# A second product of layer 2 by seven block products, with tokens in halves and two groups of PSUM banks that change parts

## The chip, the cores and the metric

The kernel runs on one core of one Trainium2 chip. The metric is device time in microseconds, the median over several runs. The engines are named as in the profile: PE (TensorE, the matmuls; PEld its weight loads), DVE (VectorE), ACT (ScalarE), POOL (GpSimd) and SP (SyncE, which issues most DMAs).

## The reference

Attention over 4 batches of 8 heads (576 tokens, head size 64) keeps only scores within tau of a row's maximum. Its output, 2304 tokens of 512 features, goes through two feed-forward layers with d_ff = 2048. q, k, v are float32; the weights of both layers arrive in 64 bits.

```python
scores = scale * np.matmul(q, k.transpose(0, 1, 3, 2))
thresh = np.max(scores, axis=-1, keepdims=True) - tau
scores = np.where(scores >= thresh, scores, -1000000000.0)
...
x = attn_out.transpose(0, 2, 1, 3).reshape(B * S, H * D)
h = x @ w_in;  r = np.maximum(h, 0.0);  x = (r * r) @ w_out      # layer 1
h = x @ w_in;  g = np.maximum(0.01 * h, h);  out = g @ w_out     # layer 2
```

## The kernel before

Attention runs first, 144 steps of one tile of queries each (functions `step`, `rest`, `values`). Between its matmuls stands the first part of layer 1 (`ffn`), 256 tokens at a time over 12 of the 16 blocks of d_ff. When attention is done, the second part of layer 1 (`h_unit`, `y_unit`) runs with 512 tokens at a time: the last 512 tokens over all of d_ff, and the rest over the remaining four blocks. Layer 2 comes last.

Layer 2 works on blocks of tokens: four of 512 and one of 256. d_ff is taken in eight pairs p of 128-wide blocks. Every operand is scaled by a power of two and split into a high and a low float16 half, and a product is three matmuls: high by high, high by low, low by high. The first product of layer 2 (`h_unit2`, line 986) already uses a scheme with seven block products in place of eight: the matrices are cut into 2 x 2 blocks, sums and differences of the blocks are multiplied, and the results are added up. Per (block, p) it has 7 products of 2 x 3 matmuls. Its four PSUM banks a, c, d, b are filled, copied or added out by ACT and DVE (lines 991 and 994), and a, c and d are added onto a second time. The activation is done by ACT on the result (lines 1014 and 1015), once to float16 and once in place, and DVE takes the difference as the low half (line 310).

The second product (`y_unit2`, line 1048) is plain: for each of four groups of 128 tokens (two in the small block) and each of the two halves of the pair, three matmuls of 512 columns, all accumulated over the eight pairs in four PSUM banks; at the last pair ACT scales a bank out (line 1052) and SP stores it.

The weights of layer 2 are loaded, converted from 64 bits, scaled and split while the second part of layer 1 runs (`single`, `bound`, `w_in2`, `w_out2`); `w_in2` also makes the sums and differences of blocks, `w_out2` only splits. `x_load2` reads layer 1's result back from DRAM, scales it and makes the seven blocks of x.

Nothing of this is in the order of the code: each call adds operations to a `Plan`, with priorities, buffers and, for some, several engines to choose from. `Plan.order` sorts them into one fixed order per engine by a table of costs (`price`, and the functions `act`, `dve`, `mm`), and each engine then works through its queue in that order.

## Time and profile before

| | us |
|---|---|
| median of 3 runs | 1037.73 |
| lowest and highest run | 1036.74, 1037.76 |
| the profiled execution | 1040.98 |
| its span in the trace | 1039.2 |
| PE busy (matmuls) in the span | 1001.7 |
| DVE, ACT, POOL busy | 714.4, 679.3, 370.4 |

The profiled execution is 3.25 us longer than the median. Busy times are unions over the span; idle time of an engine costs something only where another waits for it. The stages, as the trace shows them: attention with the first part of layer 1 until about 518 us, the second part of layer 1 until about 687 us, layer 2 until the end.

### The profile page before, as it was taken

To read this page: it belongs to the slowest core of one execution; us is meant where nothing else is said; L and a number is where in the kernel's file an instruction comes from. 1 tells how busy PE (TensorE), PEld (TensorE's weight loads), DVE (VectorE), ACT (ScalarE), POOL (GpSimd) and SP (SyncE) were. 2 spreads that over 40 slices of the span, in tenths; PEclk is the share of its full clock that TensorE was granted. 3 is DMA by queue.
4 is the path that set the end of the run, shared out by engine and by line. 5 is a ranking of instruction groups with operands and counts; after the bars stand their busy time and mean duration, and the time that the engine had idled before them with its cause. 6 is when DMAs were issued, how large, how long until landed. Compare 5 with 4: busy or idle time off the path is not lost.

```text
span 1039.2 us, 19111 instructions
## 1 busy us (share of the span) xinstructions
PE 1001.7 (96%) x6835; PEld 788.6 (76%) x6835; DVE 714.4 (69%) x1589; ACT 679.3 (65%) x1280; POOL 370.4 (36%) x482
## 2 busy tenths in 40 slices
PE   7899899999989989999999999999999999999998
PEld 4555588888989889899988898876666666666665
DVE  5988649879999877873766699996346346335333
ACT  5877787977776788875666697875455455444344
POOL 5787777975866878861200000000000000000000
PEclk9999999999999999999999999999999999999999
DMA  6554538988889996976576554331011010010010
GB/s 179 155 149 134 161 87 155 201 145 182 171 155 184 148 180 131 154 118 183 165 218 196 176 181 161 120 104 42 1 41 42 1 42 21 1 42 1 1 42 21
DMA packets 186990, 119.25 MB, mean 115 GB/s; under 512 B 146064, under 2 KB 164624, under 8 KB 186896
## 3 DMA queue, kind: packets, MB, share of 16 engines
q1 hardware_dynamic: 186528, 117.82, 48.1%
q8 instruction: 54, 0.88, 0.3%
q14 instruction: 40, 0.33, 0.1%
q10 hardware_dynamic: 368, 0.21, 0.1%
HBM read 70.98 MB, written 17.83 MB: 85 GB/s over the span
## 4 chain that ended last, share of the span: by engine, by line
PE 60%; DMA 2%; ACT 1%; POOL 0%; issue 0%; DVE 0%; DVEq 0%; ACTq 0%; POOLq 0%
PE y L1048 18%; PE h L986 16%; PE y L1109 8%; PE h L1067 8%; PE h L716 4%; PE y L742 4%; DMA PT<-P 2%; PE o L663 1%; PE s L565 1%; ACT e L576 0%; DVE e L582 0%; ACT r L723 0%; ACT tmp L678 0%; PE h L882 0%; ACT P L299 0%
## 5 line engine op out<-in xcount | busy, mean ns | idle before, releaser
L576 ACT ACTIVATE e<-s,nb 128x576 f32<-128x576 f32 x144 | 105.9, 740 | 57.7 <-DVE nb L575 38.1
L565 PE MATMUL s<-KH,Q 128*128 128x288 f32 (+1 forms) x440 | 123.3, 374 | 13.9 <-DVE e L582 9.8
L575 DVE TENSOR_REDUCE nb<-s 128x1 f32<-128x576 f32 x144 | 107.5, 750 | 33.6 <-PE s L565 32.9
L582 DVE SCALAR_TENSOR_TENSOR e<-s,th,e 128x576 f32<-128x576 f32 x144 | 116.7, 811 | 18.0 <-ACT e L576 11.4
L565 PEld LDWEIGHTS s<-KH,Q 128*128 128x128 f32 (+1 forms) x440 | 74.6, 186 | 33.0 <-issue 10.6
L1048 PEld LDWEIGHTS <-gl 128*128 128x128 f16 x432 | 42.3, 98 | 51.0
L875 POOL MEMSET xl<- 128x128 f32 x5 | 1.0, 205 | 221.8 <-issue 78.2
L629 DVE SCALAR_TENSOR_TENSOR P<-e,r,P 128x576 f16<-128x576 f32 x78 | 72.9, 943 | 7.2 <-ACT P L596 3.6
L1048 PEld LDWEIGHTS <-gh 128*128 128x128 f16 x432 | 41.9, 98 | 42.3
L663 PE MATMUL o<-PT,V 128*128 128x320 f16 (+1 forms) x396 | 57.5, 287 | 7.7 <-DVE xs L683 3.0
L565 PE MATMUL s<-KL,Q 128*128 128x288 f32 x200 | 55.8, 294 | 0.0
L663 PEld LDWEIGHTS <-V 128*128 128x128 f16 x396 | 35.4, 98 | 19.2 <-issue 6.6
L1014 ACT ACTIVATE gh<-r 128x512 f16<-128x512 f32 (+1 forms) x40 | 23.5, 588 | 40.1 <-DVE r L994 39.8
L312 POOL TENSOR_TENSOR gl<-r,gh 128x512 fp32r<-128x512 f32 x33 | 45.5, 1378 | 10.4 <-ACT gh L299 10.3
L310 DVE TENSOR_TENSOR xl<-xr,xh 128x512 f16<-128x512 f32 (+3 forms) x61 | 41.5, 684 | 10.9 <-ACT xh L299 10.5
L577 POOL TENSOR_SCALAR th<-nb,ca 128x1 f32<-128x1 f32 x85 | 36.2, 426 | 34.6 <-DVE nb L575 30.2
L1015 ACT ACTIVATE r<-r 128x512 f32<-128x512 f32 (+1 forms) x80 | 46.9, 586 | 2.2
L991 ACT COPY b0ih<-h 128x256 f32<-128x256 f32 (+1 forms) x40 | 14.0, 350 | 52.1 <-PE h L986 51.8
L994 DVE TENSOR_TENSOR b0ol<-h,b0oh 128x256 f32<-128x256 f32 (+1 forms) x20 | 7.9, 397 | 56.4 <-PE h L986 56.4
L585 POOL TENSOR_SCALAR t<-sum 128x1 f32<-128x1 f32 x82 | 33.9, 413 | 34.5 <-DVE e L582 29.7
L299 ACT CAST xh<-xr 128x512 fp32r<-128x512 f32 (+3 forms) x61 | 35.2, 582 | 15.1 <-DVE xr L310 10.8
L299 ACT CAST gh<-r 128x512 fp32r<-128x512 f32 (+1 forms) x66 | 40.3, 611 | 4.2 <-DVE r L1075 3.0
(919 smaller groups left out, 3281.1 us busy)
## 6 DMA issues: line engine op xcount, KB each, us to landing
wraw<-w SPq DMA_DIRECT2D x64, 512.0 KB, 4.4
wraw<-qT SPq DMA_DIRECT2D x20, 288.0 KB, 4.1
wraw<-kT SPq DMA_DIRECT2D x20, 288.0 KB, 4.2
out<-yo SPq DMA_DIRECT2D x18, 256.0 KB, 2.0
VA<-vv SPq DMA_DIRECT2D x32, 128.0 KB, 2.8
x2d<-yo SPq DMA_DIRECT2D x16, 256.0 KB, 2.7
xr<-x2d SPq DMA_DIRECT2D x4, 1024.0 KB, 5.4
y1d<-ys SPq DMA_DIRECT2D x14, 256.0 KB, 2.5
```

Of the source, the lines that this page charges most:

```text
L299: alts.append(("A", act(n, psum), lambda: nc.scalar.copy(o(), i()), kind))
L565: nc.tensor.matmul(ps.get()[r, g, 0:S2], lhsT=o.Q.get()[:, q], rhs=(kk.get() if o.KL else f32(kk.get()))[:, g_(g)], start=k == 0 or not o. ...
L575: op(("V", 0.75, lambda: nc.vector.tensor_reduce(out=nb.get(), in_=pv(), axis=AX.XY, op=ALU.max, negate=True)), [ps], [nb], i + CFG["pd1"] ...
L576: op(("A", 0.74, lambda: nc.scalar.activation(e.get(), pv(), AF.Exp, bias=nb.get(), scale=1.0)), [ps, nb], [e], i + CFG["pex"], True)
L582: op(("V", 0.82, lambda: nc.vector.scalar_tensor_tensor(out=e.get(), in0=pv(), scalar=th.get(), in1=e.get(), op0=ALU.is_ge, op1=ALU.mult, ...
L629: op(("V", 0.8, lambda: nc.vector.scalar_tensor_tensor(out=lo(), in0=ev(), scalar=r_.get()[:, k:k + 1], in1=hi(), op0=ALU.mult, op1=ALU.su ...
L663: nc.tensor.matmul(ps.get()[:, 0:w], lhsT=o.V16.get()[:, k if k < NH else k - NH, h].rearrange("p a d -> p (a d)"), rhs=parts16(pt)[:, k, ...
L986: nc.tensor.matmul(ps.get()[:, 0:w], lhsT=half(wt)[:, c0 + kc * P:c0 + (kc + 1) * P], rhs=xt(k)[:, kc], start=fresh and q == 0, stop=q == ...
L1015: op(("A", act(n), lambda rv=rv: nc.scalar.activation(rv(), rv(), AF.Prelu, scale=GK, alpha=0.01)), [r], [r], pr)
L1048: nc.tensor.matmul(y.get()[:, 0:DM], lhsT=l, rhs=r, start=(first and a == 0 and q == 0), stop=(last and a == 1 and q == 2))
L1067: nc.tensor.matmul(ps.get()[:, 0:n], lhsT=a.get()[:, kc * P:(kc + 1) * P], rhs=x.get()[:, kc, 0:n], start=(q == 0 and kc == 0), stop=(q == ...
L1109: nc.tensor.matmul(o(), lhsT=l, rhs=r, start=(first and q == 0), stop=(last and q == 2))
```

## The change

The second product of layer 2 also becomes seven block products. For 256 tokens and a pair p, g is a 2 x 2 matrix of blocks of 128 tokens by 128 of d_ff, and w_out a 2 x 2 matrix of blocks of 128 of d_ff by 256 features. Three of the blocks of g and three of the weights are used as they are, and four sums and differences of each are made (`h_unit2` for g, `spread` for the weights, which now serves both weight matrices). Seven products of three matmuls of 256 columns are accumulated over all eight pairs into seven half banks of four PSUM banks; only at the end are they joined, by one activation of ACT and seven operations of DVE, to two tiles of 128 tokens.

A block of 512 tokens is two such halves s of 256 tokens, and together they need eight banks, while the first product needs four of the eight that there are. So the first half is accumulated while the first product runs, in the other group of four banks, two pairs behind it; the blocks of g of the second half are kept in SBUF for all eight pairs (`g_tiles`, in tiles that are free by then), and the second half runs behind the last first product, in the banks that it used. Then the two groups change parts for the next block. The blocks of x are made between (`x_load2`, the scale now earlier in `x_stat`), into one buffer that is free only when the block's last first product is done. The activation is one instruction in place for each (block, p). The numbers of the planner's table are others, and `wold` has a third entry; GK, a power of two, keeps the sums of blocks in the range of float16.

In the diff, long lines stand whole and other parts are left out.

```diff
-GK = 2.0 ** -6
+GK = 2.0 ** -8
...
-           {'V': 2.331, 'A': 0.3, 'G': 0.438},
-           {'V': 2.518, 'A': 1.239, 'G': 2.454}],
+           {'V': 2.871, 'A': 0.393, 'G': 0.481},
+           {'V': 2.901, 'A': 1.503, 'G': 2.396},
...
+    def spread(p, g, y, keep, alone, mix, labels, fit, pr):
...
+        x0, sh, sl = (tile_of(room.pop(0)) for _ in range(3))
+        if p % 2 == 0:
+            rare[g] = tile_of(room.pop(0))
+        x2, c2 = rare[g], p % 2 * DM
+        quarter = lambda k: lambda: f32(y[k // 2].get())[:, k % 2 * h:(k % 2 + 1) * h]
+        halves((x0, 0), (x0, 2 * h), lambda: f32(y[keep].get()), 2 * h, [y[keep]], pr)
+        halves((x2, c2), (x2, c2 + h), quarter(alone), h, [y[alone // 2]], pr)
+        for o_, a_, b_, alu in mix:
+            op(tt(quarter(o_), quarter(a_), quarter(b_), h, alu), [y[a_ // 2], y[b_ // 2]], [y[o_ // 2]], pr)
         for k in range(2):
+            halves((sh, 2 * k * h), (sl, 2 * k * h), lambda k=k: f32(y[k].get()), 2 * h, [y[k]], pr)
+        room.extend(f"w{p}{'io'[g]}{k}" for k in "hl")
...
-        hi, lo = (tile_of(room.pop(0)) for _ in range(2))
-        for a, v in enumerate(y2v[1, p]):
-            op(fitted(lambda v=v: f32(v.get()), DM, fit), [v, fit], [v], pr)
-            halves((hi, a * DM), (lo, a * DM), lambda v=v: f32(v.get()), DM, [v], pr)
+        WO[p] = spread(p, 1, y2v[1, p], 1, 0, [(0, 1, 0, ALU.subtract), (1, 3, 1, ALU.subtract), (3, 3, 0, ALU.subtract), (2, 2, 3, ALU.subtract)], ("23", "1", "5746"), fit, pr)
...
+    def g_tiles(j, p, s):
+        if s == 0:
+            hi, lo = val("fb", "gh2", 3, [P, TB], F32R), val("fb", "gl2", 3, [P, TB], F32R)
+            return lambda: half(hi), lambda: half(lo), hi, lo
+        if p < 3:
+            t = val("stage", "wraw", CFG["wrb"], [P, 2 * S], F32)
+            return lambda: half(t)[:, 0:2 * DM], lambda: half(t)[:, 2 * DM:4 * DM], t, t
+        if p == 3:
+            hi, lo = (val("fb", "ya", 2, [P, TB], F32) for _ in range(2))
+            return lambda: half(hi), lambda: half(lo), hi, lo
...
-        op(tt(lambda: r2.get()[:, hi], u2, tm, w, ALU.add), [u2v, tmv, f], [r2], pr)
-        out = []
-        for r, ring in ((r1, "gh2"), (r2, "gl2")):
-            g = val("fb", ring, 3, [P, TB], F32R)
-            rv = lambda r=r: r.get()[:, 0:n]
-            op(("A", act(n), lambda g=g, rv=rv: nc.scalar.activation(half(g)[:, 0:n], rv(), AF.Prelu, scale=GK, alpha=0.01)), [r], [g], pr)
-            op(("A", act(n), lambda rv=rv: nc.scalar.activation(rv(), rv(), AF.Prelu, scale=GK, alpha=0.01)), [r], [r], pr)
-            op(sub(lambda g=g: half(g)[:, TB:TB + n], rv, lambda g=g: half(g)[:, 0:n], n), [r, g], [g], pr)
-            out.append(g)
-        G2[j, p] = out
...
+        op(tt(dest(1, 1), ta, tb, w, ALU.add), [av, bv, e], [r], pr)
+        ns = 1 + two
+        allr, alls = (lambda v=v: v.get()[:, 0:ns * 4 * P].rearrange("p (s k q) -> p s k q", s=ns, k=4) for v in (r, sv))
+        op(("A", act(ns * 4 * P), lambda: nc.scalar.activation(r.get()[:, 0:ns * DM], r.get()[:, 0:ns * DM], AF.Prelu, scale=GK, alpha=0.01)), [r], [r], pr)
+        a21, a11, a22, a12 = (lambda k=k: allr()[:, :, k] for k in range(4))
+        s1, s2, s3, s4 = (lambda k=k: alls()[:, :, k] for k in range(4))
+        op(tt(s1, a21, a22, ns * P, ALU.add), [r], [sv], pr)
+        op(sub(s3, a11, a21, ns * P), [r], [sv], pr)
+        op(sub(s2, s1, a11, ns * P), [r, sv], [sv], pr)
+        op(sub(s4, a12, s2, ns * P), [r, sv], [sv], pr)
+        p3, p7 = slice(0, 3 * P), slice(3 * P, 7 * P)
+        for s in range(ns):
+            hi, lo, hv, lv = g_tiles(j, p, s)
+            ps_ = pr + CFG["sp"] * s
+            br = lambda s=s: r.get()[:, s * DM + P:(s + 1) * DM]
+            sr = lambda s=s: sv.get()[:, s * DM:(s + 1) * DM]
+            op(rnd(lambda hi=hi: hi()[:, p3], br, 3 * P, engs="AVG"), [r], [hv], ps_)
+            op(rnd(lambda hi=hi: hi()[:, p7], sr, 4 * P, engs="AVG"), [sv], [hv], ps_)
+            op(sub(lambda lo=lo: lo()[:, p3], br, lambda hi=hi: hi()[:, p3], 3 * P), [r, hv], [lv], ps_)
+            op(sub(lambda lo=lo: lo()[:, p7], sr, lambda hi=hi: hi()[:, p7], 4 * P), [sv, hv], [lv], ps_)
+            G2[j, p, s] = hi, lo, [hv] if lv is hv else [hv, lv]
...
-            for m in range(nm):
-                Y[m] = val("ps_y", "y", 4, [P, 512], F32)
-        for m in range(nm):
-            y = Y[m]
-            for a, g in enumerate(gs):
-                def prod(m=m, a=a, g=g, y=y):
-                    gh, gl = (half(g)[:, k * TB + m * P:k * TB + (m + 1) * P] for k in range(2))
-                    vh, vl = (half(t)[:, a * DM:(a + 1) * DM] for t in (wh, wl))
+            pool, ring = banks[bank]
+            YS[j, s] = [val(pool, ring, 4, [P, 512], F32) for _ in range(4)]
+        ps = YS[j, s]
+        for y, ks in zip(ps, ("16", "72", "45", "3")):
+            vs = list(dict.fromkeys(t for k in ks for t in (WO[p][k][0], WO[p][k][2])))
+            def prod(y=y, ks=ks):
+                for c, k in enumerate(ks):
+                    wh, c0, wl, c1 = WO[p][k]
+                    gh, gl = (g()[:, piece[k] * P:(piece[k] + 1) * P] for g in (hi, lo))
+                    vh, vl = half(wh)[:, c0:c0 + h], half(wl)[:, c1:c1 + h]
                     for q, (l, r) in enumerate(((gh, vh), (gh, vl), (gl, vh))):
-                        nc.tensor.matmul(y.get()[:, 0:DM], lhsT=l, rhs=r, start=(first and a == 0 and q == 0), stop=(last and a == 1 and q == 2))
-                op(("T", 3 * mm(DM), prod), [wh, wl, g], [y], pr)
-            if last:
-                yo = val("fb", "yo", 2, [P, TB], F32)
-                op([("A", act(DM, True, True), lambda y=y, yo=yo: nc.scalar.activation(yo.get(), y.get(), AF.Copy, scale=us.get())),
-                    ("V", dve(DM, ap=True), lambda y=y, yo=yo: nc.vector.tensor_scalar(out=yo.get(), in0=y.get(), scalar1=us.get(), scalar2=None, op0=ALU.mult))], [y, us], [yo], pr)
-                dma(lambda m=m: out[t0 + m * P:t0 + (m + 1) * P, :], lambda yo=yo: yo.get()[:, 0:DM], [yo], [], pr, P * DM * 4)
+                        nc.tensor.matmul(y.get()[:, c * h:(c + 1) * h], lhsT=l, rhs=r, start=first and c == 0 and q == 0, stop=last and c == len(ks) - 1 and q == 2)
+            op(("T", 3 * len(ks) * mm(h), prod), vs + gv, [y], pr)
+        if not last:
+            return
+        top, low = (val("fb", "yo", 2, [P, TB], F32) for _ in range(2))
+        b0, b1, b2, b3 = ps
+        part = lambda t, c: lambda: t.get()[:, c * h:(c + 1) * h]
+        def join(o, ov, y, c, x, xv):
+            op(("V", dve(h, ap=True), lambda: nc.vector.scalar_tensor_tensor(out=o(), in0=part(y, c)(), scalar=us.get(), in1=x(), op0=ALU.mult, op1=ALU.add)), [y, us, xv], [ov], pr)
+        op(("A", act(h, True, True), lambda: nc.scalar.activation(part(top, 0)(), part(b0, 0)(), AF.Copy, scale=us.get())), [b0, us], [top], pr)
+        join(part(top, 1), top, b0, 1, part(top, 0), top)
+        join(part(low, 0), low, b1, 0, part(top, 1), top)
+        join(part(top, 0), top, b1, 1, part(top, 0), top)
+        join(part(low, 1), low, b2, 1, part(low, 0), low)
+        join(part(top, 1), top, b2, 1, part(top, 1), top)
+        join(part(low, 0), low, b2, 0, part(low, 0), low)
+        join(part(top, 1), top, b3, 0, part(top, 1), top)
+        r0 = t0 + s * 2 * P
+        for k, t in enumerate((low, top)):
+            dma(lambda k=k: out[r0 + k * P:r0 + (k + 1) * P, :], lambda t=t: t.get(), [t], [], pr, P * DM * 4)
...
+    for j in range(len(blocks)):
+        two, more = blocks[j][1] == TB, j + 1 < len(blocks)
+        for p in range(NU + 2):
+            if more and p == CFG["xp"]:
+                x_stat(j + 1, T0 + 2 * t, banks[bh])
+            if p < NU:
+                need(WI, p, t)
+                h_unit2(j, p, T0 + 2 * t, bh)
+                t += CFG["th"] * (2 if two else 1)
+            if p > 1:
+                need(WO, p - 2, t)
+                y_unit2(j, p - 2, 0, T0 + 2 * t, by)
+                t += CFG["th"]
+        if more:
+            x_load2(j + 1, T0 + 2 * (t - CFG["x2l"]))
+        if two:
+            for p in range(NU):
+                y_unit2(j, p, 1, T0 + 2 * t, bh)
+                t += CFG["th"]
+            bh, by = by, bh
```

Where the instructions stand. First PE in layer 2 of before, inside a step of the second block: the end of the first product (h banks) and the start of the second (y banks); gh and gl are tiles of g, w1ih, w1oh and so on tiles of weights.

```order
L986 LDWEIGHTS w1il
L986 MATMUL h_10952<-xh_9710,w1il 128x256
L1048 LDWEIGHTS gh_10900
L1048 MATMUL y<-w1oh,gh_10900 128x512
L1048 LDWEIGHTS gh_10900
L1048 MATMUL y<-w1ol,gh_10900 128x512
```

Each load serves a matmul of 512 columns. Now PE inside a second product of the changed kernel, in its first block (w2ol, w3ol and w4oh hold weights, gh and gl the high and low halves of g's blocks).

```order
L1133 LDWEIGHTS gh_9616
L1133 MATMUL y<-w2ol,gh_9616 128x256
L1133 LDWEIGHTS gl_9674
L1133 MATMUL y<-w2ol,gl_9674 128x256
L1133 LDWEIGHTS gh_9616
L1133 MATMUL y<-w3ol,gh_9616 128x256
L1133 LDWEIGHTS gh_9616
L1133 MATMUL y<-w4oh,gh_9616 128x256
```

The matmuls of the second product are 256 wide and alternate between high and low tiles of g. The change of parts of the banks: PE at the end of the first block, where the second half ends in h banks (its g kept in xl_9697) and the first product of the second block begins in y banks.

```order
L1133 LDWEIGHTS xl_9697
L1133 MATMUL h_9798<-r_8969,xl_9697 128x256
L1055 LDWEIGHTS w8ih
L1055 MATMUL y<-xh_9741,w8ih 128x256
L1055 LDWEIGHTS w8ih
L1055 MATMUL y<-xh_9741,w8ih 128x256
L1055 LDWEIGHTS w8ih
L1055 MATMUL y<-xl_9762,w8ih 128x256
```

Three first products follow here, 126 matmuls, before the first second product of that block. Next DVE in one step of before, in the second block: b0il is a tile of partial sums, r the result of the first product, gh and gl the tiles of g.

```order
L994 TENSOR_TENSOR b0il<-h_9572,b0ih 128x256
L994 TENSOR_TENSOR r_9602<-h_9588,b0ih 128x256
L994 TENSOR_TENSOR r_9602<-h_9563,b0il 128x256
L994 TENSOR_TENSOR r_9616<-h_9572,b0il 128x256
L310 TENSOR_TENSOR r_9616<-b0il 128x256
L310 TENSOR_TENSOR gh_9611<-r_9602,gh_9611 128x512
L310 TENSOR_TENSOR gl_9623<-r_9616,gl_9623 128x512
```

That is five operations of 256 columns and two of 512. DVE in one step of the changed kernel's second block: b_9016 and b_9059 are two wide tiles that hold partial sums and the blocks of g, wraw is one of the tiles in which the second half's g is kept.

```order
L1063 TENSOR_TENSOR b_9016<-y,b_9016 128x256
L329 TENSOR_TENSOR gl_10212<-b_9059,gh_10162 128x384
L329 TENSOR_TENSOR gl_10212<-b_9016,gh_10162 128x512
L329 TENSOR_TENSOR wraw<-b_9059,wraw 128x384
L1063 TENSOR_TENSOR b_9059<-y,b_9016 128x256
L329 TENSOR_TENSOR wraw<-b_9016,wraw 128x512
L329 TENSOR_TENSOR b_9016<-b_9059 128x2x128
L1063 TENSOR_TENSOR b_9059<-y,b_9016 128x256
L329 TENSOR_TENSOR b_9016<-b_9059 128x2x128
L1063 TENSOR_TENSOR b_9059<-y,b_9016 128x256
L329 TENSOR_TENSOR b_9016<-b_9016,b_9059 128x2x128
L329 TENSOR_TENSOR b_9059<-b_9016 128x256
```

Steps are interleaved here: a step has 4 additions from PSUM, 1 sum, 4 block sums (2x128 columns each; the last follows below these rows), and for each half a subtraction of 384 and one of 512. Counted over the whole order: of the pieces of layer 2's weights on DVE, 30 of 512 and 33 of 256 columns stood between the start of layer 1's second part and the first addition of layer 2, and 35 and 59 stand there now; behind it 10 and 7 stood, and 13 and 21 stand now. In attention, PE's order is the same row by row until the second product with w10 of `ffn`'s fourth block of tokens, which the trace of before has at about 425 us. Of attention's steps, POOL makes the low half of P by a subtraction (line 312) in 27 instead of 17, DVE by its fused operation (line 629) in 69 instead of 78.

## Rows read from the trace of the kernel before

**Rows 1.** Windows: length, busy us of PE, PEld, DVE, ACT, POOL; clock, DMA share, GB/s
```profile
0.00:345.00 345.00, 317.86 (x2175) 256.37 (x2176) 289.01 (x666) 259.47 (x455) 254.34 (x332) 0.99 0.74 157
345.00:400.00 55.00, 51.15 (x405) 47.83 (x405) 42.40 (x98) 43.01 (x75) 43.76 (x56) 1.00 0.93 173
...
518.00:687.00 169.00, 169.00 (x818) 141.81 (x818) 135.85 (x278) 125.35 (x255) 4.63 (x10) 1.00 0.54 170
687.00:1036.00 349.00, 348.33 (x2511) 231.69 (x2509) 162.89 (x378) 168.55 (x346) 1.81 (x5) 1.00 0.07 25
```

**Rows 2.** Waits of PE, 345 to 520 us (us in total, times, longest)
```profile
PE s L565 <- DVE e L582: 2.0, 4, 0.7
...
PE y L742 <- POOL gl L312: 0.3, 1, 0.3
```

**Rows 3.** Chain that ended last (start us, us, what)
```profile
697.06 4.58 PE h L986 x42
701.64 5.18 PE y L1048 x24
...
998.20 2.35 PE h L986 x42
1000.54 2.59 PE y L1048 x12
```

**Rows 4.** Costliest groups: weight loads of the two products (busy, mean ns)
```profile
L1048 PEld LDWEIGHTS <-gl 128*128 128x128 f16 x432 | 42.3, 98 | 51.0
...
L986 PEld LDWEIGHTS <-w0ih 128*128 128x128 f16 x80 | 7.3, 98 | 0.7
```

**Rows 5.** Timeline of PE (start us, us, instruction, count)
```profile
716.21 0.38 PE L1048 MATMUL y<-w0oh,gl 128*128 128x512 f16 x1
716.42 0.38 PE L986 MATMUL h<-xh,w1ih 128*128 128x256 f16 x2
716.64 0.38 PE L986 MATMUL h<-xl,w1ih 128*128 128x256 f16 x2
```

**Rows 6.** Timeline of DVE, queued back to back
```profile
672.40 0.68 DVE L310 TENSOR_TENSOR xl<-xr,xh 128x512 f16<-128x512 f32 x1
673.00 0.68 DVE L1075 SCALAR_TENSOR_TENSOR r<-h,r 128x512 f32<-128x512 f32 x1
...
682.29 0.42 DVE L310 TENSOR_TENSOR w6il<-w6ih,w6il 128x256 f32<-128x256 f32 x1
682.62 0.42 DVE L310 TENSOR_TENSOR w7il<-w7il 128x256 f32<-128x256 f32 x1
```

**Rows 7.** Groups by shape: activation, copy, PSUM join of 256
```profile
L1015 ACT ACTIVATE r<-r 128x512 f32<-128x512 f32 x64 | 40.2, 628 | 1.7
...
L991 ACT COPY b0ih<-h 128x256 f32<-128x256 f32 x32 | 11.9, 371 | 45.9 <-PE h L986 45.9
...
L683 DVE SCALAR_TENSOR_TENSOR xs<-o,vback,tmp 64x256 f32<-64x256 f32 x22 | 10.4, 472 | 2.5 <-ACT tmp L678 2.5
...
L1015 ACT ACTIVATE r<-r 128x256 f32<-128x256 f32 x16 | 6.7, 416 | 0.5
```

**Rows 8.** Windows of the second part of layer 1
```profile
520.00:600.00 80.00, 80.00 (x356) 66.31 (x356) 50.58 (x90) 50.36 (x109) 1.34 (x2) 1.00 0.65 195
600.00:680.00 80.00, 80.00 (x403) 67.88 (x402) 77.53 (x170) 68.94 (x134) 3.09 (x8) 1.00 0.45 147
```

**Rows 9.** Groups by shape: the low half of P
```profile
L629 DVE SCALAR_TENSOR_TENSOR P<-e,r,P 128x576 f16<-128x576 f32 x78 | 72.9, 943 | 7.2 <-ACT P L596 3.6 <-POOL P L595 3.3
...
L312 POOL TENSOR_TENSOR P<-e,P 128x576 f16<-128x576 f32 x17 | 22.5, 1321 | 3.8 <-ACT P L299 2.7 <-DVE P L301 0.4
```

**Rows 10.** End of the chain (start us, us, what)
```profile
1035.34 0.03 issue
1035.37 0.69 ACT yo L1052
```

**Rows 11.** Stores of the result (count, KB, us to landing)
```profile
out<-yo SPq DMA_DIRECT2D x18, 256.0 KB, 2.0
```

More of the change, by code (lines that the diff above doesn't have):

```diff
@@ L335, in w_block @@
         parts = []
+        whole = val(pool, tag, 1, [P, 4 * DM], F32R) if tag in ("b0", "b1") else None
+        piece = lambda k: whole.part(lambda t: t[:, k * DM:(k + 1) * DM])
         for g, io in enumerate("io"):
-            wh = val(pool, f"{tag}{io}h", 1, [P, DM], F32R)
-            wl = val(pool, f"{tag}{io}l", 1, [P, DM], F32R)
+            wh, wl = (piece(2 * g + k) if whole else val(pool, f"{tag}{io}{'hl'[k]}", 1, [P, DM], F32R) for k in range(2))
             parts.append((wh, wl))
@@ L1021, in y_unit2 @@
+    piece = {"1": 0, "4": 1, "2": 2, "5": 3, "6": 4, "7": 5, "3": 6}
+    YS = {}
+    def y_unit2(j, p, s, pr, bank):
         t0, n = blocks[j]
         first, last = p == 0, p == NF // 2 - 1
-        wh, wl = WO[p]
-        gs = G2.pop((j, p))
-        nm = n // P
-        if first:
+        hi, lo, gv = G2.pop((j, p, s))
+        h = DM // 2
+        if j not in US:
             back = X[2, j][3]
@@ L1127, in tile_kernel @@
     items = items[:n2]
-    xq = [(1, j) for j in first] + [(2, j) for j in range(len(blocks))]
+    xq = [(1, j) for j in first] + [(2, first[0])]
     def x_next(pr):
         layer, j = xq.pop(0)
-        x_load(layer, j, pr) if layer == 1 else x_load2(j, pr)
+        if layer == 1:
+            x_load(layer, j, pr)
+        else:
+            x_stat(j, pr, banks["h"])
+            x_load2(j, pr)
     x_next(T0 - 10)
```

218 lines of the change are left out of this document (121 added, 97 removed).

## The prediction, made before the changed kernel ran

> **What bounds the kernel now.** I read the windows of busy time first, then the waits of TensorE (PE), then the chain that ended last. In the first 345 us PE idles 345 - 317.86 = 27.1 us, in the 55 us behind them 3.9; from 518 to 687 (second part of layer 1) it is busy 169.00 of 169.00, and from 687 to 1036 (layer 2) 348.33 of 349; the granted clock is 0.99 to 1.00, the 2.4 GHz level, in all of them [rows 1]. The seven waits of PE that the trace names from 345 to 520 sum to 6.3 us [rows 2], and behind 520 it names none. So behind 520 the end is set by how much PE has to do, and by nothing else. VectorE (DVE) is busy 162.89 of these last 349 us, ScalarE (ACT) 168.55, GpSimd (POOL) 1.81 [rows 1].
>
> In layer 2 a step is one pair (block of 512 tokens, pair of d_ff blocks): the first product, 42 matmuls of 256 columns, takes 4.58 us, and the second, 24 of 512 columns, 5.18 us [rows 3]: 9.76 us a step, 32 such steps. In the block of 256 tokens the first product takes 2.35 us and the second 2.59 us, 8 times [rows 3].
>
> **The change on PE.** The second product becomes seven block products of three matmuls each, 256 columns wide, for each half of 256 tokens: 2 x 7 x 3 = 42 matmuls instead of 24 of 512. That is the shape and the count of the first product, so I price it by that row: 2 x 2.29 = 4.58 us. A step falls by 5.18 - 4.58 = 0.60 us, 32 times: 19.2 us. In the small block 12 matmuls of 512 become 21 of 256: 2.59 - 2.29 = 0.30 us, 8 times: 2.4 us. Together **-21.6 us**. The first product keeps its matmuls, and layer 1 and attention keep theirs.
>
> What could spoil this price is the load of the stationary operand: each matmul now loads 128 columns for 256 moved instead of 512. Loads take 98 ns each in both lines [rows 4]. A matmul of 512 columns takes its place in the queue for 0.21 to 0.22 us (5.18 / 24), and so do two of 256, each with a load of its own [rows 5]: the load is out of the way at both widths, and halving the width costs 1% a column (4.58 / 42 = 0.109 against 0.216 / 2), which is in the 4.58 us. The Trainium skill (TensorE: Matmul & The Clock Gate, section Back-to-back issue gap) speaks against the change here: it gives about 131 ns a matmul for a sustained stream of load and matmul at 512 columns and about 81 ns at 128. By a straight line between these, an estimate from that page, 256 columns would take 98 ns, and a step would go from 24 x 131 = 3.1 us to 42 x 98 = 4.1 us, which would make the kernel some 35 us slower. The trace disagrees with both figures: 216 ns at 512 columns, half of it at 256. The sum goes by the trace.
>
> **The change on DVE and ACT.** A step of before has five additions of 256 columns and two subtractions of 512 on DVE (they stand in the section on the change). After, it has nine of 256 columns (four from PSUM, one sum, four that form the blocks of g) and, for each half, one of 384 and one of 512. Queued back to back, 512 columns start 0.60 us apart and 256 columns 0.33 to 0.34 [rows 6]; 384 is put between them, 0.47. So 9 x 0.336 + 2 x (0.47 + 0.60) = 5.2 us a step instead of 5 x 0.336 + 2 x 0.60 = 2.9. On ACT: three copies, one activation of 1024 columns, and two casts of 384 and 512 for each half. Activations take 0.416 us at 256 columns and 0.628 at 512, a copy of 256 0.37 [rows 7], so I put 1024 at 1.05 and 384 at 0.51: 1.1 + 1.05 + 2 x (0.51 + 0.62) = 4.4 us. PE needs 4.58 + 2.29 = 6.87 us for a step's first product and first half, and 2.29 more for the second half, which comes only behind all eight steps. So DVE has 5.2 us of work against 6.87, of which the second half's 1.07 us may wait. Over a block it is 8 x 5.2 = 41.6, plus the next block's preparation (7 + 4 operations of 512, 6.6 us), plus 14 joins of the PSUM banks at 0.47 as for a like operation [rows 7] (6.6 us): 55 us against 8 x 9.16 = 73 us. PE's own work still hides it all.
>
> The first block is tighter. The second weights too are now spread into seven blocks. By DVE's order, behind the first addition of layer 2 stand 13 pieces of 512 and 21 of 256 columns of weights: 13 x 0.60 + 21 x 0.336 = 14.9 us; 55 + 15 = 70 of 73 us. Ahead of it stand 35 and 59 where there were 30 and 33: 5 x 0.60 + 26 x 0.336 = 11.7 us more, in layer 1, where DVE is already busy 77.53 of the last 80 us but only 50.58 of the 80 before [rows 8]. That room covers 11.7 us if the pieces come early.
>
> What a late DVE costs PE no row of layer 2 shows. Below, nothing: a gain is excluded, since PE has no idle time there to give back. Above, the rate of the first 345 us, 27.1 us of PE idle with DVE busy 289 of 345 [rows 1]: over layer 2's 327 us, 26 us. The nearer row is 600 to 680: DVE 77.53 of 80 and PE 80.00 of 80 [rows 8], in queues of the same planner and with the same kinds of waits. I take near the low end, **+1.5 us**: the gaps should lie where three first products follow each other without a second between them (each block's start), because there a PSUM bank has only two products, 1.3 us, to be read out.
>
> **Attention.** Batch four sends nine fewer fused operations to DVE (78 to 69, 0.943 us each) and ten more subtractions to POOL (17 to 27, 1.321 us each) [rows 9]; up to about 425 us PE's order is row by row the same. PE's waits from 345 on are 6.3 us, so no more can be gained; at the idle rate of the first 345 us the 173 us would hold 13.6, so 7.3 may be lost. DVE is relieved by 8.5 us and POOL, busy 43.76 of 55 [rows 1], gets up to 13: I take **0**.
>
> **The tail.** Before, the last matmul ends at 1035.34, ACT's copy of the last bank at 1035.37 + 0.69 = 1036.06, and a store of some 2 us follows [rows 10, 11]. After, one activation and seven joins in series on DVE, at 0.47 us each. The first bank is whole three more banks' matmuls ahead of the end, 1.64 us, so the chain of 8 x 0.47 = 3.8 us ends 2.1 us behind the last matmul instead of 0.7 us; part of the spacing overlaps, so **+1.0 us**, from 0 to 1.4.
>
> **Sum.** On the profiled execution: 1040.98 - 21.6 + 1.5 + 0 + 1.0 = 1021.9 us. The median of the runs lies 3.25 us under that execution (1037.73), and so I forecast **1018.6 us**.
>
> **Rivals.**
> *The static queues run late (1028 us).* In the first block DVE is at 70 of 73 us, and the order is fixed ahead. If each of the 36 full steps' worth of work (32 and 8 halves) waits 0.3 us, one addition of 256 columns in front of the awaited one, 10.8 us go: 1018.6 - 1.5 + 10.8 = 1028. For it: DVE's load in layer 2 goes from 162.89 us to about 163 + 36 x 2.3 + 63 x 0.47 = 275 of 327. Against: from 600 to 680 it is loaded more than that, and PE does not wait [rows 8]. 8%.
> *Layer 1 pays (1028 us).* If none of the 11.7 us of extra pieces finds room ahead of 600, and DVE is as full as from 600 to 680 [rows 8], layer 2 starts some 10 us later: 1028. Against it: 29 us of room from 520 to 600. 5%.
> *Slower than before (1049 us).* Each first product accumulates a second time onto three of its banks, after ACT or DVE has read them; the time for that is three products, 3 x 4.58 / 7 = 1.96 us. ACT has in its queue now an activation of 1.05 us and a cast of 0.62. If a copy stands behind both, it is done 1.05 + 0.62 + 0.37 + about 0.2 for the signals = 2.25 us after its product, 0.3 us too late; at all three that is 0.9 us a step, 32 us in 36: 1018.6 - 1.5 + 32 = 1049. It decides from 0.6 us a step on, where the gain is gone. Against it: the queues are sorted by times like those of the trace. 4%.
> *Narrow matmuls cost more a column than their row says (1038 or more).* It would need 0.6 us on 42 matmuls, 14 ns each; the spacing of 256-wide matmuls [rows 5] leaves nothing of the kind. The rule of the Trainium skill above would be of this sort. 1%.
>
> **How the numbers follow.** 82% for the forecast, whose own range is 1013 to 1024 (stalls 0 to 4, attention -3 to +3, tail 0 to 1). The two cases at 1028 hold 13%, the two at 1038 and above 5%. The range of 8 in 10 is 1013.5 to 1028. What a measurement can tell is 0.2%, 2 us: faster 0.94, the same 0.02, slower 0.04.
>
> **What would show it.** PE's second product in chains of 21 at 2.29 us; layer 2 some 327 us long with PE idle under 3 us; the start of layer 2 within 3 us of 684; DVE at 260 to 280 us of work in layer 2; the waits of PE behind 520 few and short. I am wrong if PE's waits in layer 2 sum to over 6 us, if 21 matmuls take over 2.35 us, or if attention ends more than 4 us elsewhere.

## The result, and the profile after

The changed kernel takes 1028.29 us (median of 4 runs, 1026.78 to 1029.31), the kernel before, run beside it, 1037.74: a ratio of 0.9908, 95% interval 0.9891 to 0.9925. It is 9.45 us faster; 19.1 were forecast, and 1028.29 lies just above the range's 1028.0.

The windows of the profile after, which answer to [rows 1]:

```profile
core 0: us, PE busy (x) PEld busy (x) DVE busy (x) ACT busy (x) POOL busy (x), PEclk, DMA share, GB/s
0.00:345.00 345.00, 315.61 (x2155) 254.25 (x2156) 291.98 (x664) 257.48 (x453) 253.72 (x331) 0.99 0.72 156
345.00:400.00 55.00, 51.95 (x411) 48.46 (x410) 42.73 (x98) 44.86 (x81) 44.81 (x56) 1.00 0.91 174
520.00:687.00 167.00, 166.00 (x783) 138.63 (x783) 137.24 (x285) 131.15 (x274) 3.58 (x7) 1.00 0.51 168
687.00:762.00 75.00, 74.06 (x674) 65.71 (x673) 71.32 (x174) 46.68 (x96) 2.48 (x6) 1.00 0.15 53
762.00:1021.00 259.00, 258.67 (x2531) 233.53 (x2528) 200.50 (x525) 132.33 (x287) 4.35 (x13) 1.00 0.07 23
```

PE is full again behind attention, but not wholly: a microsecond is missing at the end of layer 1 and one in the first block of layer 2 (687 to 762). The chain that ended last, which answers to [rows 3, 10]:

```profile
521.66 11.81 PE h L1166 x52
...
730.36 2.29 PE y L1133 x21
732.65 4.58 PE h L1055 x42
...
1014.33 5.25 PE y L1133 x48
...
1019.65 0.48 ACT yo L1143
...
1020.74 0.54 DVE yo L1142 x2
...
1021.53 0.93 DVE yo L1142 x3
```

A half of the second product takes 2.29 us, as forecast. The first row is a landmark that both kernels have, some 4 us into the second part of layer 1. The same two places in the chain of before:

```profile
518.59 11.81 PE h L1067 x52
...
1030.15 5.19 PE y L1048 x24
```

The same 52 matmuls start at 518.59 before and at 521.66 after, so attention ends 3.07 us later. The last matmul starts at 1034.95 before, 1020.93 after: from the landmark to it 516.36 and 499.27, 17.09 less. From its start to the span's end (1039.2 and 1026.5) it was 4.25 us and is 5.6.

Where PE waited behind attention, by the waits and by its timeline (the second fence, in brackets its idle time):

```profile
PE y L1208 <- DVE gl L329: 1.0, 1, 1.0
PE h L1055 <- ACT b L1060: 0.7, 1, 0.7
PE h L1055 <- DVE b L1063: 0.2, 1, 0.2
```

```profile
683.14 0.49 PE L1208 MATMUL y<-gh,b3oh 128*128 128x512 f32 x1
684.60 0.50 PE L1208 MATMUL y<-gl,b3oh 128*128 128x512 f32 x1 [0.97 <-DVE gl L329]
...
697.79 0.38 PE L1055 MATMUL h<-xh,w10il 128*128 128x256 f16 x2
698.88 0.38 PE L1055 MATMUL h<-xh,w10ih 128*128 128x256 f16 x2 [0.72 <-ACT b L1060]
```

The first lies at layer 1's last second product, the second in the third pair of the first block, where three first products follow each other. ACT's queue shows why its copy came late there: it stood behind a cast of g that waited 0.89 us for a sum of DVE.

```profile
697.94 0.62 ACT L318 CAST gh<-b 128x512 f16<-128x512 f32 x1 [0.89 <-DVE b L329]
698.47 0.37 ACT L1060 COPY b<-h 128x256 f32<-128x256 f32 x1
```

Shorter ones don't show as waits, so I also worked out PE's **lost time**: over all matmuls from layer 1's second part on, the distance of each start to the next less the median distance of its line and shape, summed. It is 0.15 us before and 4.68 after.

### The profile page after: what moved, and what is told of

It is laid out like the page before. It is cut to its first block, busy times and chain, and to the rows that moved or that the text cites. A ratio compares the mean times of both kernels' runs of the same rounds, so it can differ in the third digit from the quotient of the medians.

```text
span 1026.5 us, 20798 instructions
## 1 busy us (share of the span) xinstructions
PE 982.9 (96%) x7483; PEld 852.0 (83%) x7483; DVE 828.3 (81%) x1926; ACT 699.4 (68%) x1347; POOL 377.9 (37%) x489
## 4 chain that ended last, share of the span: by engine, by line
PE 65%; DVE 13%; ACT 7%; DMA 6%; issue 5%; POOL 4%; SPq 0%; DVEq 0%; POOLq 0%; ACTq 0%
PE y L1133 8%; PE h L1166 8%; PE y L1208 7%; PE h L1133 7%; PE y L1055 7%; PE h L1055 6%; PE y L762 5%; PE s L585 5%; PE h L736 5%; DMA PT<-P 4%; DVE e L602 3%; PE o L688 2%; DVE nb L595 2%; PE o L683 2%; DVE P L649 2%
## 5 line engine op out<-in xcount | busy, mean ns | idle before, releaser
L602 DVE SCALAR_TENSOR_TENSOR e<-s,th,e 128x576 f32<-128x576 f32 x144 | 116.7, 811 | 15.5 <-ACT e L596 11.7
L649 DVE SCALAR_TENSOR_TENSOR P<-e,r,P 128x576 f16<-128x576 f32 x69 | 66.4, 970 | 7.3 <-ACT P L616 5.6
L1133 PEld LDWEIGHTS <-gh 128*128 128x128 f16 x560 | 54.5, 98 | 6.2
L1082 ACT ACTIVATE b<-b 128x1024 f32<-128x1024 f32 (+1 forms) x40 | 38.8, 971 | 29.7 <-DVE b L329 29.5
L318 ACT CAST gh<-b 128x384 f16<-128x384 f32 (+1 forms) x76 | 42.7, 563 | 21.7 <-DVE b L329 21.0
L329 DVE TENSOR_TENSOR b<-b 128x256 f32<-128x256 f32 (+1 forms) x120 | 45.8, 394 | 13.4 <-ACT b L1082 13.0
L318 ACT CAST xh<-xr 128x512 fp32r<-128x512 f32 (+3 forms) x66 | 37.5, 580 | 21.6 <-DVE xr L329 15.5
L329 DVE TENSOR_TENSOR gl<-b,gh 128x384 f16<-128x384 f32 x80 | 49.2, 621 | 0.2 <-ACT gh L318 0.2
L318 ACT CAST gh<-r 128x512 fp32r<-128x512 f32 (+1 forms) x71 | 43.0, 606 | 3.9 <-DVE r L1174 2.7
L605 POOL TENSOR_SCALAR t<-sum 128x1 f32<-128x1 f32 x77 | 31.3, 406 | 35.3 <-DVE e L602 29.5
L1063 DVE TENSOR_TENSOR b<-h,b 128x256 f32<-128x256 f32 (+1 forms) x96 | 35.9, 378 | 5.4 <-PE h L1055 3.6
```

Source lines behind the costliest of these rows:

```text
L318: alts.append(("A", act(n, psum), lambda: nc.scalar.copy(o(), i()), kind))
L329: alts.append(("V", dve(n), lambda: nc.vector.tensor_tensor(out=o(), in0=a(), in1=b(), op=alu), kind + "*"))
L602: op(("V", 0.82, lambda: nc.vector.scalar_tensor_tensor(out=e.get(), in0=pv(), scalar=th.get(), in1=e.get(), op0=ALU.is_ge, op1=ALU.mult, ...
L649: op(("V", 0.8, lambda: nc.vector.scalar_tensor_tensor(out=lo(), in0=ev(), scalar=r_.get()[:, k:k + 1], in1=hi(), op0=ALU.mult, op1=ALU.su ...
L1133: nc.tensor.matmul(y.get()[:, c * h:(c + 1) * h], lhsT=l, rhs=r, start=first and c == 0 and q == 0, stop=last and c == len(ks) - 1 and q == 2)
```

## Experiments

"Lost" is that sum, in us; "stretch" is the time from layer 1's second part's first matmul to the last one (520.32 before, 503.23 after).

### The same kernels again

> The changed kernel again, unchanged, with five rounds. Seen so far: 1028.29 us, 9.45 below the kernel before, where 19.1 were forecast; in its trace the start of the second part of layer 1 is 3.1 us late, the stretch from there to the end of layer 2's first block 3.8 us above its matmuls, the tail 1.45 us longer. Theory P (these places belong to the kernel): the same three numbers within 0.5 us, and 1028.3 +- 0.7. Theory N (part of them is run-to-run spread: the granted clock had a dip at 339 to 343 us in that profile, and the profile of before lay 3.25 us above its median): the attention number changes by 1 to 3 us in this second profile.

> The kernel before again, unchanged, with a profile of its own. Theory P: attention ends at 518.6 us again, and the profiled execution lies some 3 us above the median because the profile itself costs that. Theory N: attention's end moves by 1 to 3 us between profiles of one kernel, and the profiled execution lies within 1 us of the median this time; then the 3.25 us that the prediction took off did not belong to the changed kernel.

Measured: the changed kernel 1029.67 us against 1039.23 (ratio 0.9907, 0.9886 to 0.9928), the kernel before 1039.53 (1.0003, 0.9990 to 1.0016). The stretch is 503.23 and 520.32 again, to 0.01 us: behind attention a kernel does the same each time. The landmark moves (changed kernel first, then before):

```profile
524.71 11.81 PE h L1166 x52
```

```profile
516.97 11.81 PE h L1067 x52
```

So theory P holds behind attention, and theory N in it. The profile of before that the prediction went by was 2 us late already at its 22nd microsecond, which no later profile of any kernel repeats; this time the profiled execution took 1039.41, no more than the median. The forecast compares medians (1037.73 - 19.1), so the 3.25 us that it took off are no part of the miss. Part of N is the granted clock. Windows of the two profiles of the changed kernel, first and again:

```profile
330.00:340.00 10.00, 7.96 (x61) 7.62 (x60) 7.42 (x17) 4.67 (x10) 3.35 (x6) 0.97 1.18 194
339.00:343.00 4.00, 4.00 (x21) 3.72 (x21) 4.00 (x10) 3.04 (x6) 3.45 (x5) 0.57 0.31 57
```

```profile
66.00:71.00 5.00, 2.52 (x14) 1.82 (x14) 4.86 (x11) 3.48 (x7) 3.52 (x5) 1.00 0.25 55
71.00:76.00 5.00, 4.71 (x21) 2.79 (x23) 2.85 (x10) 1.91 (x3) 3.97 (x5) 0.66 0.89 268
```

The clock falls to its lower level, 1.2 GHz, for some 3.4 us (0.57 of full speed over 4 us, 0.66 over 5), each time behind a stretch in which PE had waited (2.0 us up to 338.6; 3.0 us in three waits from 66 to 71): the waits cost a second time, some 1.1 us at 339 and 1.6 at 71 (by how far PE's matmuls there fall behind the same ones of before).

### Attention

e1 sets attention's numbers back: two rows of `price`, `lb`, the priorities, two switches (`xu`, `hu`), the two numbers by which the planner holds an engine free, and the four that time layer 1's weights (here with a copy of `wo` for attention alone). The edits in this section are shortened.

```diff
-    lead1=0.796, lb=[[5, 7], [1, 5], [4], [1, 4, 6, 7]], pd1=1.15, pex=1.456, pd2=1.281, ph=3.708, pl=-3.081,
-    w0=25.596, wstep=1.439, wo=1.97, wold=[9, 10, 16], ...
+    lead1=0.809, lb=[[1, 2, 3, 4, 5, 7], [1, 5], [4], [4, 6]], pd1=0.327, pex=1.205, pd2=1.197, ph=3.26, pl=-2.11,
+    w0=24.975, wstep=1.452, wo0=3.465, wold=[9, 10], ...
```

> The changed kernel with the planner's numbers for attention as they were before, so that every engine's order up to the end of attention is that of the kernel before. Theory A (the new numbers cost 3 us in attention, by DVE reaching the sum over e later): attention's end comes back to 518.6 +- 0.5 and the time falls by 2.5 to 3.5 us against the changed kernel, to some 1025. Rival: the 3 us are spread between runs or come from the clock: within 1 us of the changed kernel's 1028.3. Second rival: the numbers were chosen for what follows: attention ends 3 us earlier, but the second part of layer 1 starts with its weights and transfers as late as before and gives it back, 1028.

> e1 again, to stand beside e7 on one chip and to see whether its 1024.05 us hold. Theory: 1024 +- 1.5, the stretch from the second part of layer 1 to the last matmul 503.2 us again. Rival (e1's gain was chance between runs): 1027 or more.

b1 is the converse: the kernel before with the new numbers, all but the two of the holds. Up to about 490 us its trace has the operations of PE, DVE, ACT and POOL in the changed kernel's order.

> The kernel before, with the changed kernel's numbers for attention and nothing else of the change; every engine's order is that of the changed kernel up to the end of attention. Theory A (these numbers cost attention some 5.6 us, whatever layer 2 does): 1039.2 + 4 to 6 = 1043 to 1045 us, slower than before beyond the interval. Rival (they cost only in company with the changed layer 2): 1038 to 1040.

Measured: e1 1024.05 us (ratio to before 0.9856, 0.9839 to 0.9874), again 1025.48 (0.9862, 0.9843 to 0.9882); b1 1045.3 (1.0055, 1.0040 to 1.0070), **5.6 us slower** than before with nothing else changed. The landmarks of e1 and b1:

```profile
515.84 11.81 PE h L1167 x52
```

```profile
525.11 11.81 PE h L1067 x52
```

It lies at 515.8 to 520.2 in the twelve profiles with the old numbers, those of later experiments among them, and at 521.7 to 525.1 in the four with the new (the mean moves by 5.7 us). Theory A holds from both sides, with 5.6 us where e1 was expected to gain 2.5 to 3.5; the second rival falls, since e1's stretch is 503.21.

One place shows how. DVE and POOL of the changed kernel (start, duration), then DVE and POOL of the kernel before again:

```profile
60.06 2.12 DVE L372 TENSOR_SCALAR wraw<-wraw 128x512 int32<-128x512 int32 x1
62.10 0.80 DVE L602 SCALAR_TENSOR_TENSOR e<-s,th,e 128x576 f32<-128x576 f32 x1
...
63.50 1.62 DVE L374 SCALAR_TENSOR_TENSOR wraw<-wraw 128x512 int32<-128x512 int32 x1
```

```profile
59.59 0.85 POOL L701 TENSOR_TENSOR xs<-xs,tmp 64x320 f32<-64x320 f32 x1
60.43 1.47 POOL L615 TENSOR_SCALAR e<-e,r 128x576 f32<-128x576 f32 x2
```

```profile
60.88 0.41 DVE L352 TENSOR_SCALAR wraw<-wraw 128x512 int32<-128x512 int32 x1
...
62.92 0.68 DVE L354 SCALAR_TENSOR_TENSOR wraw<-wraw 128x512 int32<-128x512 int32 x1
```

```profile
59.94 0.85 POOL L681 TENSOR_TENSOR xs<-xs,tmp 64x320 f32<-64x320 f32 x1
61.14 1.48 POOL L595 TENSOR_SCALAR e<-e,r 128x576 f32<-128x576 f32 x2 [0.34 <-DVE r L588]
```

The same shift takes 0.41 us or 2.12. Before, it starts as POOL pauses for 0.34 us; in the changed kernel it is queued a little earlier against POOL, whose three operations run from 59.59 to 61.90 without a pause, and it ends 0.28 us behind them. The reduction of e, for which a score product waits, stands behind it. The Trainium skill ("SBUF — State Buffer", section "Who interferes with whom") says that VectorE in some modes and GpSimd hold a shared pair of ports exclusively, and that the other blocks fully. These rows agree. e8 sets only the four weight numbers back:

```diff
-    w0=25.596, wstep=1.439, wo=1.97, wold=[9, 10, 16]
+    w0=24.975, wstep=1.452, wo0=3.465, wold=[9, 10]
```

> The changed kernel, with the four numbers that time layer 1's weight conversions in attention (w0, wstep, wo, wold) as before: TensorE's order stays that of the changed kernel, and DVE, ACT and POOL have the order of before up to some 330 us. At 60 us of the changed kernel one shift on DVE takes 2.12 us instead of 0.41 while POOL runs two scalings back to back (1.47 us), and a score product waits 1.3 us behind it; at 63.5 us a second one takes 1.62 instead of 0.68. Theory W (that meeting of DVE and POOL is the loss at 64 to 74 us): that place gains 1.9 us, the places at 327 to 340 and 400 to 428 us stay: some 1026.5. Rival (the meeting happens anyway, or the place moves): within 0.7 us of the changed kernel.

Measured: 1026.17 us (0.9870, 0.9851 to 0.9888), and the two operations:

```profile
60.75 0.41 DVE L372 TENSOR_SCALAR wraw<-wraw 128x512 int32<-128x512 int32 x1
62.80 0.68 DVE L374 SCALAR_TENSOR_TENSOR wraw<-wraw 128x512 int32<-128x512 int32 x1
```

Theory W holds at its place: the loss at 64 to 74 us, 2.2 us in the first profile, is gone, by the matmuls that both kernels share. In b1 the operations take 2.13 and 1.61. The whole gain, 0.9870 against 0.9908 and 0.9907, is some 3.8 us, twice the expected one; the intervals allow either. The list `lb` alone, set back in the changed kernel (e5) or forward in e1 (e6):

```diff
-lb=[[5, 7], [1, 5], [4], [1, 4, 6, 7]]
+lb=[[1, 2, 3, 4, 5, 7], [1, 5], [4], [4, 6]]
```

> The changed kernel, with only the list of attention steps that take the unfused path (lb) as before, which sends nine subtractions of batch four back from POOL to DVE's fused form. In the traces the changed kernel loses some 1.9 us at 64 to 74 us, 2.5 us at 327 to 340 us and 1.2 us at 400 to 428 us, each in front of a score product that waits for DVE. Theory L (the list costs it): only the third place can gain, by 1 us at most, since the list changes nothing ahead of some 345 us: 1027 to 1028. Rival (the list causes all): attention's end 4 to 6 us earlier, 1023 to 1024.

> The converse: e1 (attention's numbers as before) but with the changed kernel's list lb. Theory (the other numbers, by which weight conversions and transposing transfers are queued, cost the 1.9 and 2.5 us; the list costs 1.2 us at most): within 1.5 us of e1's 1024.05. Rival: 1028 or more.

Measured: e5 1031.39 us (0.9927, 0.9904 to 0.9950), e6 1027.34 (0.9885, 0.9858 to 0.9911). By the medians I missed both: the old list gains nothing among the new numbers (0.9927 against 0.9907), and the new one costs 2 to 3 us among the old (0.9885 against 0.9856 and 0.9862), where I gave it 1.2 at most. The intervals overlap, so neither is clear of noise. How the rest of the 5.6 us splits among the numbers stays open.

### Layer 2: how much work DVE has

e2 leaves out w_out's sums (in the changed kernel, so its time holds attention's loss), e9 (on e1) both matrices' sums, e4 (on e1) does w_out's twice.

```diff
-        for o_, a_, b_, alu in mix:
+        for o_, a_, b_, alu in mix if g == 0 else ():          # e2
+        for o_, a_, b_, alu in ():                             # e9
+        for o_, a_, b_, alu in mix if g == 0 else mix + mix:   # e4
```

> The changed kernel without the 32 sums and differences of w_out's blocks (four operations of 256 columns on DVE for each of eight pairs, 32 x 0.336 = 10.8 us); the blocks are split as they are, so the output is not the reference's. The work of TensorE is the same. Theory D (at 680 to 716 us DVE is the bound, full with weight pieces, and that is what the start of layer 2 pays): the stretch from the second part of layer 1 to the end of layer 2's first block falls from 240.8 to 237 to 238 us and the time by 2.5 to 3.5 us. Rival: its gaps come from the order (an operation queued in front of the awaited one), not from how much there is: under 1 us gained.

> Built on e1, without the sums and differences of the blocks of both weight matrices (64 operations of 256 columns, 21.5 us of DVE; the output is not the reference's). Theory D (the amount on DVE from 660 to 740 us sets TensorE's lost time): it falls from 4.7 to under 2.5 us, the stretch from layer 1's second part to the last matmul from 503.2 to 501 us or less. Rival C (a chain sets it: layer 1's last activation goes ACT, DVE, ACT, DVE with only one second product to cover it, and the first x block comes late): 4 to 5 us as before, with the gap of 1.2 us at layer 1's last second product.

> Built on e1. The 32 sums and differences of w_out's blocks are done twice in place (10.8 us more on DVE; the output is not the reference's). Rival D (DVE's amount sets the gaps): with DVE full from 680 to 740 us the gaps grow by 5 to 10 us, to some 1031. Theory O (the order sets them): they stay within 1.5 us of 4.7, since DVE has room behind 740 us and ahead of 680 us.

| | work on DVE, by count | lost | stretch | time, ratio to before |
|---|---|---|---|---|
| e9 | -21.5 | 4.8 | 503.30 | 1025.04, 0.9865 (0.9836 to 0.9895) |
| e2 | -10.8 | 4.7 | 503.25 | 1029.35, 0.9917 (0.9895 to 0.9939) |
| e1 | 0 | 4.7 | 503.21 | 1024.05, 0.9856 |
| e4 | +10.8 | 17.6 | 516.12 | 1037.83, 0.9992 (0.9973 to 1.0010) |

Windows of e9, then of e4:

```profile
640.00:660.00 20.00, 20.00 (x88) 16.07 (x87) 10.11 (x18) 12.75 (x25) 0.47 (x2) 1.00 0.51 158
660.00:680.00 20.00, 19.92 (x88) 16.10 (x87) 17.41 (x37) 13.92 (x26) 0.11 (x1) 1.00 0.33 106
680.00:700.00 20.00, 18.91 (x156) 16.16 (x157) 20.00 (x44) 16.44 (x38) 0.20 (x1) 1.00 0.40 132
700.00:720.00 20.00, 19.25 (x177) 17.03 (x176) 19.92 (x56) 14.56 (x32) 2.61 (x4) 1.00 0.00 1
```

```profile
680.00:700.00 20.00, 18.22 (x141) 14.95 (x139) 20.00 (x50) 12.70 (x26) 0.20 (x1) 1.00 0.40 133
700.00:720.00 20.00, 17.07 (x154) 14.94 (x153) 18.08 (x51) 13.31 (x32) 4.15 (x4) 1.00 0.00 1
720.00:740.00 20.00, 17.42 (x147) 14.81 (x145) 20.00 (x51) 12.52 (x25) 0.00 (x0) 0.91 0.00 1
```

Less work gains nothing (theory D falls, twice): even in e9 DVE idles 12.5 us from 640 to 680 and is full in the 40 behind. The relief is less than the count, since the planner gave DVE other operations: in e9's trace it has 53 fewer than in e1's, and is busy 809.3 us instead of 825.7.

e4 loses 12.9 us more for 10.8 of work, beyond the 5 to 10 that were expected, but that doesn't show DVE to be the limit, for little of it is waiting in DVE's queue. By place, against e1: 2.8 us for an operation of POOL, 2.7 for an addition on DVE, 2.8 for pieces of w_out, whose sums are the doubled work, some 3 by two falls of the clock (0.91 from 720 to 740), the rest in small waits. POOL's operation belongs to the scale of the next x block; it takes 0.81 us in e1 and 2.96 in e4, while DVE's operations run back to back, the last ending at 712.67. In e7, below, it takes 3.55. POOL in e1, POOL in e4, and PE in e4:

```profile
704.32 0.81 POOL L903 TENSOR_SCALAR yo<-eye_sb,xlead 128x128 f32<-128x128 f32 x1 [8.87 <-DVE xlead L899]
```

```profile
709.95 2.96 POOL L903 TENSOR_SCALAR yo<-eye_sb,xlead 128x128 f32<-128x128 f32 x1 [10.21 <-DVE xlead L899]
...
712.96 0.49 PE L904 MATMUL h<-yo 128*128 128x128 f32 x2 [2.91 <-POOL yo L903]
```

So the amount of work in the first block is near what was forecast (71.32 us busy in the changed kernel's 75 from 687 to 762, for 70 of 73), but that this amount is the limit is not shown.

### Layer 2: in what order

e3 marks what PE waits for as urgent and lets the planner hold DVE and ACT for it; e7 gives the first x block scratch tiles of its own (its expectation should have said: the squares start 138.3 us behind the landmark, before 133.4; e7 brings them to 136.4 only, so it tests less than half of the delay); e10 and e11 shift all weight pieces; e12 hands out tiles in another order; e13 is e12 with e7. All are built on e1.

```diff
-tol=-0.303, hor=-0.104
+tol=0.05, hor=0.45                                        # e3, and True behind pr of the awaited operations
-        junk = val("fb", "yo", 2, [P, TB], F32)
+        own = [val("wb", f"x{k}1", 1, [P, KC, TB], F32R) for k in "hl"] if j == first[0] else []   # e7
+        junk = own[0] if own else val("fb", "yo", 2, [P, TB], F32)
-ww=21.57
+ww=31.57                                                  # e10; 11.57 in e11
-        if len(room) < need:
-            room.extend(spares or ["r2", "r2"])
-            spares[:] = []
+        while len(room) < need:                           # e12
+            room.append(spares.pop(0))
```

> Built on e1 (1024.05 us). From the second part of layer 1 to the last matmul TensorE loses 4.7 us against its own spacing, at the same places in every run (1.4 us at the last second product of layer 1, 1.1 us in the first block's third pair, 0.7 us in the small block); e2 showed that 32 fewer operations on DVE leave the sum at 4.7 us. Here the planner holds DVE and ACT free (0.45 us ahead) for the operations that TensorE waits for in layer 1's second part and in layer 2 (copies and additions out of PSUM, the low half of layer 1's activation). Theory O (order: a weight piece was started in front of the awaited operation): the 4.7 us fall under 2 us and the time to some 1021. Rival D (amount: DVE is full from 680 to 720 us whatever the order): the sum stays above 4 us, with the gaps at other pairs, since held time is lost there.

> Built on e1. In the changed kernel the first x block of layer 2 gets its maximum through the two yo buffers, which layer 1's results also use: POOL's fill of yo waits for a store, the squares start at 660.0 us where before they started 142 to 143 us ahead of that point's equivalent, and the scaled x is there 7 us later than before, so that layer 2's first product can't stand ahead of layer 1's last second product. Here that first block uses the tiles xh and xl as scratch, as before. Theory X (the gap of 1.3 us at layer 1's last second product and the bound's 0.4 us come from this): the sum of TensorE's lost time behind attention falls from 4.7 to 2.5 to 3.5 us and the time by 1.2 to 2.2 us against e1 in this same call. Rival D (DVE is full, so a gap closed here opens in the first block): within 0.5 us of e1.

> Built on e1, with the weight pieces' priority number 10 higher (ww 31.57): they give way to more of the work of their time. Theory D: DVE's total up to 762 us is the same, so TensorE's lost time stays within 3.5 to 7 us. Theory O (the pieces' place sets it): it falls under 2.5 us here or in e11. Rival: the late pieces are then waited for by the products themselves, 8 us or more.

> Built on e1, with the weight pieces' priority number 10 lower (ww 11.57). They then stand ahead of layer 1's activations and the x block. Theory D: within 3.5 to 7 us. Theory O: under 2.5 us here if they are too late in the changed kernel. Rival: layer 1's products wait for their activations, 8 us or more.

> Built on e1; only the order in which the weight pieces take their tiles is changed: freed tiles first, and of the eight tiles b2 and b3, which layer 1 reads until its end, only as many as a pair lacks. In the changed kernel w_out's second to fourth pair lie wholly in b2 and b3. Theory T (the pieces are bunched between 670 and 720 us by waiting for these tiles, and TensorE's 4.7 us of lost time follow): it falls under 3 us, the stretch from layer 1's second part to the last matmul under 501.6 us, the time by some 2 us against e1. Rival C (the chain at layer 1's end, ACT, DVE, ACT, DVE behind one second product, and layer 2's first pairs with nothing beside them): within 0.7 us of 4.7.

> e12 with e7's early x block. Theory T: with the pieces spread out, the early x block no longer opens a gap elsewhere, so both gains add: under 2 us of lost time, the stretch under 500.6 us, some 1022. Rival C or D: 4.5 us or more, as in e7, whose lost time was 6.5 us.

| | lost | stretch | time, ratio to before |
|---|---|---|---|
| e10, pieces later | 4.8 | 503.33 | 1024.97, 0.9864 (0.9834 to 0.9895) |
| e7, x early | 6.5 | 505.05 | 1024.99, 0.9858 (0.9840 to 0.9875) |
| e13, both | 5.8 | 504.31 | 1026.77, 0.9862 (0.9825 to 0.9898) |
| e12, tiles | 7.1 | 505.56 | 1025.78, 0.9860 (0.9834 to 0.9885) |
| e3, held | 10.7 | 509.19 | 1030.78, 0.9916 (0.9892 to 0.9941) |
| e11, pieces earlier | 11.7 | 510.25 | 1031.65, 0.9920 (0.9890 to 0.9951) |

e7 and e12 close the gap at layer 1's last second product: it loses under 0.3 us there instead of 1.2 to 1.3. Yet the time comes back as waits of the first product for copies and additions out of PSUM (PE's waits in e7, then e12):

```profile
PE h L1058 <- DVE b L1066: 2.5, 3, 1.9
PE y L1058 <- ACT b L1063: 0.5, 1, 0.5
```

```profile
PE h L1055 <- ACT b L1060: 1.4, 2, 0.7
PE h L1055 <- DVE b L1063: 0.9, 4, 0.3
```

Theories O, X and T fall as they were put, X by an early block that came only part of the way. What is shown: between 680 and 720 us DVE is busy at least 19.6 of each 20 us in all of these kernels but e4, a gap closed in one place opens in another, and none of the six orders loses less than 4.7 us. What causes the 4.7 us stays open: which of the arrivals (the last activations of layer 1, the x block, the weight pieces) puts so much of DVE's work behind 680 us, whether DVE's amount or the chains between ACT and DVE set the waits, and whether any order avoids them.

## Why the prediction was half right

| step | forecast | measured |
|---|---|---|
| second product on PE | -21.6 | -21.6 (the stretch's -17.1 less 4.5 of lost time) |
| PE's stalls behind attention | +1.5 | +4.5 |
| attention | 0 | +5.6 (b1; 4.2 to 7.3) |
| tail | +1.0 | +1.3 |
| sum | -19.1 | -10.2; the runs say -9.5 and -9.6 |

**The price on PE was right**, to 0.1 us in 21.6: 21 matmuls in 2.29 us, loads out of the way, as [rows 3 to 5] said. The rule in the Trainium skill ("TensorE: Matmul & The Clock Gate", section "Back-to-back issue gap") that spoke against it doesn't hold here: a matmul of 256 columns takes 0.109 us after as before (4.58 / 42), and the time went down.

**"Attention: I take 0" is the step that failed**, with 5.6 of the 9.7 us. I compared PE's order, took it to be the same up to 425 us, counted nine operations fewer on DVE, and set them against POOL's ten more. The time was misread: the product with w10 of the fourth block, where PE's order parts, runs at 361.7 to 364.9 us in the trace of before. Above all, DVE's, ACT's and POOL's orders differ from the first 60 us on, and one shift that meets POOL takes 1.7 us more. The bound of 7.3 us, from the idle rate of the first 345 us, held by luck: it was worked out for the 173 us behind 345, while by the mean of the profiles PE with the new numbers is 3.1 us later at 345 already, of 5.7 at the landmark. The forecast's own range of -3 to +3 did not use it, nor did any rival.

**The stalls were mis-sized**: 4.7 us of lost time (0.15 before) against a forecast of 1.5. By place it is 1.5 us in the first block, where three first products follow each other (the place that was forecast), and 0.9 in the small block; 1.4 at layer 1's last second product and 0.5 ahead of it, where I expected nothing; the rest is scattered, and the start of blocks two to four shows none. DVE works 71.32 + 200.50 = 271.8 us in layer 2, as forecast (260 to 280). Why these stalls are as long as they are stays open.

**The tail** is a size too: 1.3 to 1.4 us instead of 1.0, at the upper end of 0 to 1.4.

**The rivals.** *Layer 1 pays*: its second part loses 1.9 us, not ten. (The start of layer 2 measures this badly: its first matmul is at 687.28, against a forecast of 684, but before it was at 679.53, because a first product stood ahead of layer 1's last second one.) *The static queues run late*: its mechanism is there, for a few operations of the first block and not for all 36 steps. *Slower*, by a copy of ACT that comes too late: a wait that the trace names occurs once (0.72 us at 698), and the copy stands behind a cast that waits for DVE, not behind an activation and a cast. By time the two at 1028 fit, by cause neither does.

**The signs.** None of the three signs of being wrong showed in the first profile: PE lost under 3 us in layer 2, 21 matmuls took 2.29 us, and attention ended 3.07 us later, under the 4 that were set. Only the profiles taken again (524.71 against 516.97), e1 and b1 show how much attention costs: one profile of each kernel can't, when the changed kernel's own landmark moves by 3 us from one profile to the next.

e1, the changed kernel with attention's old numbers, takes 1024.05 and 1025.48 us, 1.4% below the kernel before; no kernel here is faster beyond the intervals.
